# Fourteen of eighteen 128x1024 transposes moved from TensorE to VectorE blocks and DMAs by way of HBM

## The chip, the core and the metric

The kernel runs on one core of a Trainium2 chip. The metric is the device time of one execution in microseconds (us), the median of several runs; lower is better. One further execution was profiled. The engines are named as in the profile: PE is TensorE (PEld its weight loads), DVE is VectorE, ACT is ScalarE, POOL is GpSimd, and SP is the queue from which all of this kernel's DMAs are issued. Each engine and each queue works through its own instructions in the order in which they were written.

## What is computed

Attention without softmax, then a gated MoE layer, then a second MoE layer with SoLU and a layer norm. The change is in the second MoE, for 2304 tokens, a model width of 512 and a hidden width of 1024:

```python
h = x @ w_in                                   # [2304,512] @ [512,1024]
e = np.exp(h - np.max(h, axis=-1, keepdims=True))
sm = e / (np.sum(e, axis=-1, keepdims=True) + 1e-09)
solu = h * sm
mu = np.mean(solu, axis=-1, keepdims=True)
var = np.mean((solu - mu) ** 2, axis=-1, keepdims=True)
ln = (solu - mu) / np.sqrt(var + 1e-06) * g_ln
out = ln @ w_out                               # [2304,1024] @ [1024,512]
```

Everything is float32. A product is made of three matmuls of high and low parts (high by high, high by low, low by high).

## The kernel before

The 2304 tokens are 18 tiles of 128. The first part (attention and the first MoE) leaves its result, transposed, in two SBUF tiles `ya`, one for tokens 0 to 1279 and one for the rest. The second MoE takes the tiles in nine pairs.

For each pair, `make_a` forms the seven left operands of Strassen's product (`A11` to `S4`): four additions on DVE, and for each operand a rounded high part (an ACT copy) and a low part (a POOL subtraction). `run_h` issues the seven products P1 to P7, 42 matmuls of 512 columns in all, and with them, on ACT and DVE, the copies and additions that combine them in PSUM (L942 to L960). A pair occupies two of the four PSUM slots (two banks each).

`post_h` then takes each tile of 128 tokens x 1024 features: DVE finds the maximum (L998), ACT the exponential with its sum (L999), DVE multiplies by h into the SBUF tile `u` (L1000), after which the PSUM slot is free, DVE takes the statistics (L981, L982) and subtracts the mean in place (L1003), and POOL works out the scale of each row (L987 to L992), which the very last step applies.

`run_t` transposes the tile: eight PE transposes of 128x128 (L1020) into another PSUM slot; ACT rounds the result into `dh` (L1029), and DVE subtracts that from it into the low part `dl` (L1030). `dh` and `dl` have two buffers each, the ring `R_D`. `run_o` multiplies with `w_out` (24 matmuls of 512 columns, L703 to L705), ACT scales the rows into `ot`, which has two buffers (L1048), and SP stores it (L1049).

The order of the instructions is made beforehand, by a planner in the kernel's own Python code. The class `Order` keeps a time for each engine; every step has a planned cost in microseconds and a rank, and the step that is due first by these is written next. Nothing of the plan is left when the kernel runs but the order on each engine. The loop of the second MoE chooses what PE does next: a transpose if a tile is due, then the next product of a pair if fewer than `AHEAD` tiles lie between h and out, then the output of a tile:

```python
        if i in d_ready and d_ready[i][0] <= od.now and ps_ready() <= od.now and R_D.ok():
            run_t(todo_t.pop(0))
            continue
        ...
        if h_can and (hp or ahead < AHEAD or not o_can):
            run_h()
            continue
        if o_can:
            run_o(todo_o.pop(0))
```

Of the kernel before, what the change touches and what calls it, by code (L numbers as in the profile page):

```python
# [17 lines left out]
P = 128  # L18
# [120 lines left out]
def attention_moe_moe_kernel(ctx: ExitStack, tc, kv_in, kv_tail, q_in, g_norm, w1, w_in, w_out2, g_ln, out):  # L139
# [224 lines left out]
    def store(k, f, u, su, sf, t, slot=None, raw=None):  # L364

        what, x, y = k

        def free():
            R_U.give(su)
            R_F.give(sf)  # L370
            decode_more()

        if what == "i":

            g, r = x % 2, 2 * (x // 2) + y
# [12 lines left out]
        if what == "o":  # L388

            g = gl_sb[:, x:x + 1]  # L390
            at = raw.bitcast(F32R)
            hi, lo = at[:, 0:CH], at[:, CH:2 * CH]

            def out_to(t):
                free()
                d = scr["o", x] = dr.tile([P, 2 * CH], F32, tag=f"so{x}", name=f"so{x}")
                nc.sync.dma_start(out=d, in_=raw.bitcast(F32))
                scr_at["o", x] = when = od.load(8 * CH * P) + 1.5
                od.chain([(None, 0, gone)], t=when)

            def gone(t):
                R_RAW.give(slot)
                loads()

            od.chain([
                ("T", 1.32, lambda: nc.gpsimd.tensor_tensor(out=f, in0=f, in1=u, op=ALU.add)),
                ("A", 0.7, lambda: nc.scalar.activation(out=hi, in_=f, func=AF.Copy, scale=g)),
                ("S", 0.7, lambda: nc.vector.scalar_tensor_tensor(
                    out=lo, in0=f, scalar=g, in1=hi.bitcast(F32), op0=ALU.mult, op1=ALU.subtract)),
                (None, 0, out_to),  # L410
            ], rank=5, t=t)
# [421 lines left out]

    R_H, R_D, R_AO = Ring(4), Ring(2), Ring(2)
    held, d_ready, dt_ready, scs = [], {}, {}, {}
    G2 = 0.68
    todo_a, todo_h, todo_t, todo_o = list(range(NTT // 2)), list(range(NTT)), list(range(NTT)), list(range(NTT))
    a_ops, a_at = {}, {}  # L840
    AT = {"A11": 0, "A12": 1, "A22": 2, "S1": 3, "S2": 4, "S3": 5, "S4": 6}
    SEQ = [("P1", "A11", B11), ("P6", "S2", T2), ("P2", "A12", B21), ("P5", "S1", T1), ("P7", "S3", T3),
           ("P3", "S4", B22), ("P4", "A22", T4)]
# [10 lines left out]
    def make_a(i, slot, when):  # L854
# [11 lines left out]
        def part(cost, d, src, last):  # L866
            n = slice(*d)

            def done(t):
                for x in range(*d):  # L870
                    a_at[i, x] = t

            od.chain([
                ("A", cost, lambda: nc.scalar.copy(out=hi[:, n], in_=src)),  # L874
                ("G", 2.15 * cost, lambda: nc.gpsimd.tensor_tensor(  # L875
                    out=lo[:, n], in0=src, in1=hi[:, n].bitcast(F32), op=ALU.subtract)),
                (None, 0, done),
            ], rank=2.5, t=max(od.now, last))

        a_ops[i] = at, slot  # L880
        part(0.6, (0, 2), first, when)
# [3 lines left out]
            (None, 0, lambda t: part(0.6, (3, 5), s[:, 0:2], t)),  # L885
            add(s[:, 2], a11, a21, ALU.subtract), add(s[:, 3], a12, s[:, 1], ALU.subtract),
            (None, 0, lambda t: part(0.6, (5, 7), s[:, 2:4], t)),
        ], rank=2.5, t=max(od.now, when))

    hp = []  # L890

    def next_h():

        if not hp:
            i = todo_h[0] // 2 if todo_h else None
            if (i not in a_ops or R_H.taken - len(R_H.given) > 2
                    or sum(t <= od.now for t in ps_free.values()) < 2):
                return INF
            return max([a_at.get((i, 0), INF)] + [b_at.get((g, B11), INF) for g in range(2)])
        p = hp[0]  # L900
# [5 lines left out]
    def run_h():  # L906
        if not hp:
            i = todo_h.pop(0)
            todo_h.pop(0)
            p = {"i": i, "n": 0, "slots": [ps_tile(f"h{i}"), ps_tile(f"h{i + 1}")], "u": [R_H.take(), R_H.take()]}  # L910
            p["a"], p["sa"] = a_ops[i // 2]
            hp.append(p)
        p = hp[0]
# [44 lines left out]
            od.chain([is_done("p7")], t=at)  # L958
        elif name == "P3":
            pre = [("V", 0.69, lambda: nc.vector.tensor_tensor(out=Z, in0=Z, in1=s1, op=ALU.add))]  # L960
            post_or_hold(p["i"], p["slots"][0], p["u"][0], pre)
        elif name == "P4":
            R_AO.give(p["sa"])
            hp.pop()
            post_or_hold(p["i"] + 1, p["slots"][1], p["u"][1], [])
            a_more()

    def post_or_hold(i, slot, sh, pre):
        if ph2 is None:
            held.append(lambda: post_h(i, *slot, sh, pre))  # L970
        else:
            post_h(i, *slot, sh, pre)

    def post_h(i, slot, ps, sh, pre):
        u = ph2.tile([P, 2, 512], F32, tag="u", name=f"u{i}", bufs=4)
        st = ph2.tile([P, 24], F32, tag="st", name=f"st{i}", bufs=6)
        nmax, ssum, mv, sv, sc = st[:, 0:1], st[:, 1:2], st[:, 4:6], st[:, 6:7], st[:, 7:8]

        def stats():
            for n in range(2):  # L980
                nc.vector.bn_stats(out=st[:, 12 + 6 * n:18 + 6 * n], in_=u[:, n, :])  # L981
            nc.vector.bn_aggr(out=mv, in_=st[:, 12:24])  # L982

        def root():


            nc.gpsimd.tensor_scalar(out=ssum, in0=ssum, scalar1=1e-9, scalar2=None, op0=ALU.add)  # L987
            nc.gpsimd.tensor_tensor(out=sv, in0=ssum, in1=ssum, op=ALU.mult)
            nc.gpsimd.tensor_scalar(
                out=sv, in0=sv, scalar1=1e-6, scalar2=mv[:, 1:2], op0=ALU.mult, op1=ALU.add  # L990
            )
            nc.gpsimd.tensor_tensor(out=sc, in0=sv, in1=mhalf[:, 0:1], op=ALU.pow)  # L992

        def ready(t):
            d_ready[i] = (t, u, sh)

        od.chain(pre + [
            ("V", 1.13, lambda: nc.vector.tensor_reduce(out=nmax, in_=ps, axis=AX.XY, op=ALU.max, negate=True)),  # L998
            ("A", 1.09, lambda: nc.scalar.activation(out=u, in_=ps, func=AF.Exp, bias=nmax, accum_out=ssum)),  # L999
            ("V", 1.14, lambda: nc.vector.tensor_tensor(out=u, in0=ps, in1=u, op=ALU.mult)),  # L1000
            ps_done(slot),
            ("V", 1.4, stats),
            ("V", 0.66, lambda: nc.vector.tensor_scalar(  # L1003
                out=u, in0=u, scalar1=mv[:, 0:1], scalar2=None, op0=ALU.subtract)),
            (None, 0, ready),
            ("G", 1.2, root),
            (None, 0, lambda t: scs.__setitem__(i, sc)),
        ], rank=2, t=od.now + 0.2)

    def run_t(i):  # L1010
        _, u, sh = d_ready[i]
        slot, ps = ps_tile(f"t{i}")
        sd = R_D.take()
        u, ps = (x.rearrange("p a f -> p (a f)") for x in (u, ps))
        dh = ph2.tile([P, DF2], F32R, tag="dh", name=f"dh{i}", bufs=2)
        dl = (late[0][0][:, 3584:3584 + DF2], late[0][1][:, 4096:4096 + DF2])[sd % 2]

        def go():
            for ft in range(NF2):
                nc.tensor.transpose(ps[:, ft * P:(ft + 1) * P], u[:, ft * P:(ft + 1) * P], ident)  # L1020

        od.pe(0.87, go)
        R_H.give(sh)

        def done(t):
            dt_ready[i] = (t, dh, dl, sd)

        od.chain([
            ("A", 0.9, lambda: nc.scalar.copy(out=dh, in_=ps)),  # L1029
            ("V", 1.14, lambda: nc.vector.tensor_tensor(out=dl, in0=ps, in1=dh.bitcast(F32), op=ALU.subtract)),  # L1030
            ps_done(slot),
            (None, 0, done),
        ], rank=1.5, t=od.now + 0.2)

    def run_o(i):
        _, dh, dl, sd = dt_ready[i]
# [50 lines left out]
    while any(ab) or busy or yq:  # L1087
# [48 lines left out]
            nxt.append(od.events[0][0])  # L1136
        assert nxt, "stuck"
        od.now = max(od.now, min(nxt))
    AHEAD = 4
    while todo_o:  # L1140
        od.until(od.now)
        late_loads()
# [1 line left out]
        ahead = len(todo_o) - len(todo_h)  # L1144
        h_can = next_h() <= od.now
        i = todo_t[0] if todo_t else None
        if i in d_ready and d_ready[i][0] <= od.now and ps_ready() <= od.now and R_D.ok():
            run_t(todo_t.pop(0))
            continue
        i = todo_o[0]  # L1150
# [78 lines left out]
```

## Time and profile before

| what | value |
|---|---|
| median of three runs | 706.12 us (705.1 to 706.95) |
| the profiled execution, its own time | 706.26 us |
| its span, first to last instruction | 704.5 us |
| mean granted TensorE clock | 0.998 |

The span is shorter than the execution's own time by 1.76 us, which lie outside the first and the last instruction. Busy times are sums over instructions; matmuls are pipelined, so their listed durations overlap, and the time from the start of one step to the start of the next is what a step takes of PE.

### The profile page before, as it was taken

What the parts mean: (1) busy time and instruction counts of PE and PEld (TensorE: products, weight loads), DVE (VectorE), ACT (ScalarE), POOL (GpSimd) and SP (SyncE); (2) the same over time, 40 slices, a digit from 0 to 9 for tenths busy, and PEclk for the clock granted to TensorE, in tenths of its full rate; (3) what the DMA queues carried; (4) which work ended last, traced back from release to release, by engine and by line L of the source; (5) the groups of instructions that cost most, each with busy time, mean ns of one, the idle gap of its engine ahead of it and who ended that gap; (6) DMA issues with size and microseconds to landing.
All of it is one profiled execution on the core that took longest, in us unless ns stands there. A gap on an engine that the chain in (4) does not pass through costs nothing.

```text
span 704.5 us, 9627 instructions
## 1 busy us (share of the span) xinstructions
PE 690.4 (98%) x3690; PEld 600.5 (85%) x3690; DVE 513.3 (73%) x746; ACT 262.0 (37%) x462; POOL 247.5 (35%) x243
## 2 busy tenths in 40 slices
PE   5899999999999999999999999999999999999998
PEld 5799988989898888989898989898788888888887
DVE  2889735888978899779878788565597857765560
ACT  3677534333233233232232232212354534443331
POOL 2676314342364445513232322202335433322110
PEclk9999999999999999999999999999999999999999
DMA  8974101122232121132232312013500000000001
GB/s 295 364 276 143 60 0 61 60 90 90 90 140 99 61 89 60 43 115 83 91 120 76 124 70 91 31 60 122 208 0 31 16 30 31 16 22 24 31 30 46
DMA packets 23630, 61.45 MB, mean 87 GB/s; under 512 B 4768, under 2 KB 6048, under 8 KB 23584
## 3 DMA queue, kind: packets, MB, share of 16 engines
q1 hardware_dynamic: 23584, 60.83, 24.8%
q8 instruction: 29, 0.48, 0.3%
q14 instruction: 17, 0.14, 0.1%
HBM read 48.76 MB, written 12.06 MB: 86 GB/s over the span
## 4 chain that ended last, share of the span: by engine, by line
PE 95%; DMA 3%; SPq 0%; DVE 0%; ACT 0%; issue 0%; ACTq 0%
PE y L788 21%; PE ab L703 14%; PE ab L705 14%; PE ab L704 14%; PE h L928 12%; PE out L705 5%; PE out L703 5%; PE out L704 5%; PE t L1020 2%; DMA kv<-in_kv 2%; PE o L635 2%; DMA raw_w<-in_w 1%; PE t L680 1%; PE pkv L590 1%; SPq L263 0%; DVE ya L801 0%
## 5 line engine op out<-in xcount | busy, mean ns | idle before, releaser
L703 PE MATMUL ab<-xh,wh_w 128*128 128x512 f32 (+1 forms) x480 | 177.9, 371 | 0.0
L705 PE MATMUL ab<-xh,wl_w 128*128 128x512 f32 (+1 forms) x480 | 177.0, 369 | 0.0
L704 PE MATMUL ab<-xl,wh_w 128*128 128x512 f32 (+1 forms) x480 | 176.8, 368 | 0.0
L801 DVE TENSOR_TENSOR ya<-y,ya 128x1024 f32<-128x1024 f32 (+1 forms) x110 | 122.3, 1112 | 2.2 <-PE y L788 2.1
L424 POOL TENSOR_TENSOR f_w<-f_w,wh_w 128x512 f32<-128x512 f32 x36 | 47.8, 1329 | 163.8 <-ACT wh_w L423 106.0
L757 ACT COPY a<-ab 128x512 f32<-128x512 f32 (+1 forms) x60 | 32.7, 544 | 193.8 <-PE ab L705 193.7
L758 DVE TENSOR_TENSOR ab<-ab,a 128x512 f32<-128x512 f32 (+1 forms) x60 | 38.7, 646 | 85.0 <-ACT a L757 84.8
L703 PEld LDWEIGHTS ab<-xh,wh_w 128*128 128x128 f32 x480 | 90.1, 188 | 12.2 <-issue 0.3
L704 PEld LDWEIGHTS ab<-xl,wh_w 128*128 128x128 f32 x480 | 90.2, 188 | 11.6
L705 PEld LDWEIGHTS ab<-xh,wl_w 128*128 128x128 f32 x480 | 90.1, 188 | 11.4
L788 PE MATMUL y<-gl,wh_w 128*128 128x512 f32 (+1 forms) x240 | 88.5, 369 | 0.3 <-DVE gl L760 0.3
L788 PE MATMUL y<-gh,wh_w 128*128 128x512 f32 (+1 forms) x240 | 88.8, 370 | 0.0
L788 PE MATMUL y<-gh,wl_w 128*128 128x512 f32 (+1 forms) x240 | 88.5, 369 | 0.0
L928 PE MATMUL h<-wd,lateh 128*128 128x512 f32 x216 | 58.1, 390 | 0.0
L788 PEld LDWEIGHTS y<-gl,wh_w 128*128 128x128 f32 x240 | 45.1, 188 | 6.6 <-DVE gl L760 0.8
L788 PEld LDWEIGHTS y<-gh,wh_w 128*128 128x128 f32 x240 | 45.1, 188 | 5.8
L788 PEld LDWEIGHTS y<-gh,wl_w 128*128 128x128 f32 x240 | 45.0, 188 | 5.6
L425 POOL TENSOR_TENSOR wl_w<-f_w,u_w 128x512 fp32r<-128x512 f32 x36 | 47.6, 1327 | 3.6 <-DVE u_w L345 2.2
L928 PEld LDWEIGHTS h<-wd,lateh 128*128 128x128 f32 x216 | 40.5, 188 | 8.4
L928 PE MATMUL h<-latel,lateh 128*128 128x512 f32 x162 | 46.3, 394 | 0.0
L703 PE MATMUL out<-wh_o,dh 128*128 128x512 f32 (+1 forms) x114 | 43.9, 385 | 0.0
L875 POOL TENSOR_TENSOR lateh<-ya,lateh 128x512 fp32r<-128x512 f32 (+1 forms) x18 | 18.2, 1016 | 72.6 <-ACT lateh L874 72.6
(103 smaller groups left out, 1141.7 us busy)
## 6 DMA issues: line engine op xcount, KB each, us to landing
raw_w<-in_w SPq DMA_DIRECT2D x36, 512.0 KB, 3.4
kv<-in_kv SPq DMA_DIRECT2D x16, 512.0 KB, 7.1
out<-ot SPq DMA_DIRECT2D x17, 256.0 KB, 2.0
raw_i<-in_w_in SPq DMA_DIRECT2D x8, 512.0 KB, 3.5
raw_o<-in_w_out SPq DMA_DIRECT2D x8, 512.0 KB, 3.3
so<-raw_o SPq DMA_DIRECT2D x8, 512.0 KB, 2.6
q<-in_q SPq DMA_DIRECT2D x12, 256.0 KB, 5.1
si<-wd SPq DMA_DIRECT2D x6, 512.0 KB, 2.6
```

The lines of the kernel that those rows point to most:

```text
L424: ("T", 1.32, lambda: nc.gpsimd.tensor_tensor(out=f, in0=f, in1=hi.bitcast(F32), op=ALU.subtract)),
L425: ("T", 1.38, lambda: nc.gpsimd.tensor_tensor(out=lo, in0=f, in1=u, op=ALU.add)),
L635: nc.tensor.matmul(ps[m * w:(m + 1) * w, p * P:(p + 1) * P], lhsT=src[:, m * w:(m + 1) * w], rhs=bds[b % 2][:, p], start=True, stop=True)
L703: nc.tensor.matmul(o, lhsT=ah, rhs=bh, start=first, stop=False)
L704: nc.tensor.matmul(o, lhsT=ah, rhs=bl, start=False, stop=False)
L705: nc.tensor.matmul(o, lhsT=al, rhs=bh, start=False, stop=last)
L757: ("A", 0.45 * k, lambda: nc.scalar.copy(out=a, in_=ps[:, 0, 0:nb])),
L758: ("V", 0.54 * k, lambda: nc.vector.tensor_tensor(out=g, in0=g, in1=a, op=ALU.mult)),
L788: nc.tensor.matmul(o, lhsT=x[:, s], rhs=y, start=f == fs[0] and n == 0, stop=f == fs[-1] and n == 2)
L801: op = ("V", 0.9 * nb / NB, lambda: nc.vector.tensor_tensor(out=dst, in0=src, in1=dst, op=ALU.add))
L875: ("G", 2.15 * cost, lambda: nc.gpsimd.tensor_tensor(out=lo[:, n], in0=src, in1=hi[:, n].bitcast(F32), op=ALU.subtract)),
L928: nc.tensor.matmul(o, lhsT=x, rhs=y, start=first and k == m == 0, stop=k == 1 and m == 2, skip_group_check=not first)
```

## The change

For tiles 4 to 17 (all but those in `ON_PE`) the PE transpose goes. In its place:

- DVE transposes the tile `u` in 32x32 blocks, in two instructions of 128x512, into a piece of `ya` that is no longer needed (each pair's piece joins the list `ya_free` when all seven of its operands are made). The input is read at a step of four elements.
- SP issues two stores of this piece to HBM and, behind them, two loads from there, which bring the tile back with the blocks in their transposed places: 256 KB each, in runs of 512 bytes. A load goes to another free piece of `ya`, or to `u` if none is free. The planner counts 6.0 us (`HOP`) from the stores to the data.
- ACT and DVE make `dh` and `dl` from this SBUF tile instead of from PSUM; no PSUM slot is taken.

For all 18 tiles the mean is subtracted by ACT (as mean minus value, and `g_ln` is negated once by POOL to make up for it), not by DVE. `u` is taken from its four buffers only at the exponential, and no longer at the start of the pair. `AHEAD` is 6, not 4. The making of the operands has rank 1.7 in place of 2.5, now ahead of the steps of `post_h`, which have rank 2 and a little more for each tile.

```diff
+            minus = ("G", 0.3, lambda: nc.gpsimd.tensor_scalar(out=gl_sb, in0=gl_sb, scalar1=-1.0, scalar2=None, op0=ALU.mult))
+            od.chain([minus] * (x == 0) + [
...
+    NU, PLACES = 4, 2
+    R_H, R_D, R_AO = Ring(NU), Ring(2), Ring(2)
...
+    ya_free, HOP, ON_PE = [], 6.0, (0, 1, 2, 3)
...
+                if all((i, x) in a_at for x in range(7)):
+                    ya_free.append(i)
...
-            ], rank=2.5, t=max(od.now, last))
+            ], rank=1.7, t=max(od.now, last))
...
-            if (i not in a_ops or R_H.taken - len(R_H.given) > 2
-                    or sum(t <= od.now for t in ps_free.values()) < 2):
+            if i not in a_ops or sum(t <= od.now for t in ps_free.values()) < PLACES:
...
+        def go(t):
+            if not R_H.ok():
+                od.chain([(None, 0, go)], rank=2 + 0.02 * i, t=t + 0.2)
+                return
+            sh = R_H.take()
+            u = ph2.tile([P, 2, 512], F32, tag="u", name=f"u{i}", bufs=NU)
...
+            uf = u.rearrange("p a f -> p (a f)")
+            st_u = {}
+            def blocks(h):
+                n = slice(h * 4, h * 4 + 4)
+                nc.vector.transpose(out=ya_of(st_u["b"]).rearrange("p b (f i) -> p f b i", i=32)[:, n],
+                                    in_=uf.rearrange("p (f i b) -> p f b i", b=4, i=32)[:, n])
+            def turn(t):
+                if i in ON_PE:
+                    d_ready[i] = (t, uf, lambda: R_H.give(sh))
+                    return
+                if not ya_free:
+                    od.chain([(None, 0, turn)], rank=2 + 0.02 * i, t=t + 0.2)
+                    return
+                st_u["b"] = ya_free.pop(0)
+                st_u["d"] = [dr.tile([P, 4 * P], F32, tag=f"su{i % 4}{h}", name=f"su{i}_{h}") for h in range(2)]
+                ops = []
+                for h in range(2):
+                    ops += [("V", 0.6, lambda h=h: blocks(h)), (None, 0, lambda t, h=h: off(t, h))]
+                od.chain(ops, rank=2 + 0.02 * i, t=t)
+            def off(t, h):
+                nc.sync.dma_start(out=st_u["d"][h].rearrange("p (b e) -> p b e", b=4),
+                                  in_=ya_of(st_u["b"])[:, :, h * P:(h + 1) * P])
+                if h:
+                    back_in(t)
+            def back_in(t):
+                od.chain([(None, 0, lambda t: ya_free.append(st_u["b"]))], t=t + 2.3)
+                if ya_free:
+                    n = ya_free.pop(0)
+                    to = ya_of(n)
+                    R_H.give(sh)
+                    free = lambda: ya_free.append(n)
+                else:
+                    to = uf.rearrange("p (a e) -> p a e", a=4)
+                    free = lambda: R_H.give(sh)
+                for h in range(2):
+                    nc.sync.dma_start(out=to[:, :, h * P:(h + 1) * P],
+                                      in_=st_u["d"][h].rearrange("(a j) (b e) -> (j b) a e", a=4, b=4))
+                d_ready[i] = (t + HOP, to, free)
...
+                ("A", 1.25, lambda: nc.scalar.activation(out=u, in_=ps, func=AF.Exp, bias=nmax, accum_out=ssum)),
+                ("V", 1.2, lambda: nc.vector.tensor_tensor(out=u, in0=ps, in1=u, op=ALU.mult)),
+                ps_done(slot),
+                ("V", 1.5, stats),
+                ("A", 1.09, lambda: nc.scalar.activation(out=u, in_=u, func=AF.Identity, bias=mv[:, 0:1], scale=-1.0)),
+                (None, 0, turn),
...
-            ("V", 0.66, lambda: nc.vector.tensor_scalar(
-                out=u, in0=u, scalar1=mv[:, 0:1], scalar2=None, op0=ALU.subtract)),
...
+        if i in ON_PE:
...
+        else:
+            src, freed = u.rearrange("p a (f i) -> p f a i", i=32), (None, 0, lambda t: free())
+            to = [d.rearrange("p (f a i) -> p f a i", a=4, i=32) for d in (dh, dl)]
...
+            ("A", 1.05, lambda: nc.scalar.copy(out=to[0], in_=src)),
+            ("V", 1.2, lambda: nc.vector.tensor_tensor(out=to[1], in0=src, in1=to[0].bitcast(F32), op=ALU.subtract)),
...
-    AHEAD = 4
+    AHEAD = 6
...
-        if i in d_ready and d_ready[i][0] <= od.now and ps_ready() <= od.now and R_D.ok():
+        if i in d_ready and d_ready[i][0] <= od.now and R_D.ok() and (i not in ON_PE or ps_ready() <= od.now):
```

## Rows read from the trace of the kernel before

**Rows 1.** The page: engine, busy us, share of the span, instructions.

```profile
PE 690.4 (98%) x3690; PEld 600.5 (85%) x3690; DVE 513.3 (73%) x746; ACT 262.0 (37%) x462; POOL 247.5 (35%) x243
```

**Rows 2.** The page, the chain that ended last, by engine.

```profile
PE 95%; DMA 3%; SPq 0%; DVE 0%; ACT 0%; issue 0%; ACTq 0%
```

**Rows 3.** Stretches: window, length, busy us by engine, granted clock, DMA share, GB/s.

```profile
500.40:565.00 64.60, 64.56 (x304) 53.35 (x303) 52.14 (x75) 31.05 (x51) 28.11 (x41) 1.00 0.10 37
565.00:690.00 125.00, 125.00 (x606) 104.62 (x605) 76.58 (x109) 49.41 (x74) 33.16 (x60) 1.00 0.07 26
587.50:609.70 22.20, 22.20 (x107) 18.55 (x106) 14.46 (x22) 9.69 (x15) 7.46 (x12) 1.00 0.07 25
690.00:704.50 14.50, 11.24 (x73) 10.08 (x71) 1.23 (x1) 2.68 (x5) 0.00 (x0) 1.00 0.15 54
```

**Rows 4.** The chain in order of time, one pair: start us, us, what.

```profile
572.69 9.54 PE h L928 x42
...
587.68 0.87 PE t L1020 x8
588.55 0.23 PE out L703
...
594.02 0.87 PE t L1020 x8
594.89 9.54 PE h L928 x42
```

**Rows 5.** Groups on DVE by form, 150 to 480 us: 128x512 from SBUF.

```profile
L345 DVE SCALAR_TENSOR_TENSOR u_w<-raw_w,u_w 128x512 f32<-128x512 uint32 x24 | 20.6, 860 | 0.3
...
L341 DVE TENSOR_SCALAR u_o<-f_o 128x512 uint32<-128x512 uint32 x8 | 3.4, 420 | 0.0
```

**Rows 6.** Groups on DVE, 505 to 692 us: busy us, mean ns, idle before.

```profile
L981 DVE BATCH_NORM_STATS2 st<-u 128x6 f32<-128x512 f32 x36 | 22.7, 671 | 0.0
L1003 DVE TENSOR_SCALAR u<-u,st 128x1024 f32<-128x1024 f32 x18 | 13.0, 728 | 0.0
L1030 DVE TENSOR_TENSOR latel<-t,dh 128x1024 fp32r<-128x1024 f32 x9 | 11.0, 1220 | 5.6 <-ACT dh L1029 5.5
L864 DVE TENSOR_TENSOR bt<-ya,bt 128x256 f32<-128x256 f32 x7 | 4.0, 574 | 0.0
L864 DVE TENSOR_TENSOR bt<-bt,ya 128x256 f32<-128x256 f32 x7 | 2.9, 419 | 0.0
```

**Rows 7.** Groups on ACT, the whole span.

```profile
L999 ACT ACTIVATE u<-h,st 128x1024 f32<-128x1024 f32 x18 | 20.1, 1118 | 12.3 <-DVE st L998 12.2
L1029 ACT CAST dh<-t 128x1024 fp32r<-128x1024 f32 x18 | 18.3, 1019 | 6.6 <-PE t L1020 5.1
...
L874 ACT CAST lateh<-bt 128x512 fp32r<-128x512 f32 x18 | 11.2, 624 | 20.7 <-DVE bt L864 20.5
...
L324 ACT ACT_TABLE_LOAD x1 | 1.3, 1283 | 0.7 <-PEq L1219 0.7
```

**Rows 8.** The SP queue in order of time: start us, us of issuing, instruction.

```profile
19.44 2.01 SPq L256 DMA_DIRECT2D qs<-in_q  x2
...
500.43 0.32 SPq L511 DMA_DIRECT2D wh_o<-so  x1
```

**Rows 9.** DMA issues: count, KB each, median us from issue to landing.

```profile
out<-ot SPq DMA_DIRECT2D x17, 256.0 KB, 2.0
...
so<-raw_o SPq DMA_DIRECT2D x8, 512.0 KB, 2.6
...
wh_o<-so SPq DMA_DIRECT2D x6, 256.0 KB, 2.7
...
qs<-in_q SPq DMA_DIRECT2D x4, 128.0 KB, 8.1
```

**Rows 10.** Stretches of the first part: columns as in Rows 3.

```profile
5.00:10.00 5.00, 3.10 (x42) 2.56 (x44) 2.67 (x5) 1.23 (x4) 1.37 (x2) 1.00 0.98 361
45.00:50.00 5.00, 5.00 (x38) 4.96 (x36) 4.01 (x5) 4.16 (x11) 4.53 (x3) 1.00 0.99 359
```

**Rows 11.** DVE in order of time behind one pair: start us, us, instruction.

```profile
603.84 2.36 DVE L998 TENSOR_REDUCE st<-h 128x1 f32<-128x1024 f32 x2
...
611.54 0.70 DVE L1003 TENSOR_SCALAR u<-u,st 128x1024 f32<-128x1024 f32 x1
```

More of the change, by code (lines that the diff above doesn't have):

```diff
@@ L403, in gone @@
                 loads()
-            od.chain([
+            minus = ("G", 0.3, lambda: nc.gpsimd.tensor_scalar(out=gl_sb, in0=gl_sb, scalar1=-1.0, scalar2=None, op0=ALU.mult))
+            od.chain([minus] * (x == 0) + [
                 ("T", 1.32, lambda: nc.gpsimd.tensor_tensor(out=f, in0=f, in1=u, op=ALU.add)),
@@ L830, in second @@
         held.clear()
-    R_H, R_D, R_AO = Ring(4), Ring(2), Ring(2)
+    NU, PLACES = 4, 2
+    R_H, R_D, R_AO = Ring(NU), Ring(2), Ring(2)
     held, d_ready, dt_ready, scs = [], {}, {}, {}
@@ L887, in make_a @@
             (None, 0, lambda t: part(0.6, (5, 7), s[:, 2:4], t)),
-        ], rank=2.5, t=max(od.now, when))
+        ], rank=1.7, t=max(od.now, when))
     hp = []
@@ L909, in run_h @@
             todo_h.pop(0)
-            p = {"i": i, "n": 0, "slots": [ps_tile(f"h{i}"), ps_tile(f"h{i + 1}")], "u": [R_H.take(), R_H.take()]}
+            p = {"i": i, "n": 0, "slots": [ps_tile(f"h{i}"), ps_tile(f"h{i + 1}")]}
             p["a"], p["sa"] = a_ops[i // 2]
@@ L960, in run_h @@
             pre = [("V", 0.69, lambda: nc.vector.tensor_tensor(out=Z, in0=Z, in1=s1, op=ALU.add))]
-            post_or_hold(p["i"], p["slots"][0], p["u"][0], pre)
+            post_or_hold(p["i"], p["slots"][0], pre)
         elif name == "P4":
@@ L964, in run_h, with post_or_hold @@
             hp.pop()
-            post_or_hold(p["i"] + 1, p["slots"][1], p["u"][1], [])
+            post_or_hold(p["i"] + 1, p["slots"][1], [])
             a_more()
-    def post_or_hold(i, slot, sh, pre):
+    def post_or_hold(i, slot, pre):
         if ph2 is None:
-            held.append(lambda: post_h(i, *slot, sh, pre))
+            held.append(lambda: post_h(i, *slot, pre))
         else:
[L972 to L976, printed above, removed]
+            post_h(i, *slot, pre)
@@ L977, in post_h @@
+    def post_h(i, slot, ps, pre):
+        st = ph2.tile([P, 24], F32, tag="st", name=f"st{i}", bufs=8)
         nmax, ssum, mv, sv, sc = st[:, 0:1], st[:, 1:2], st[:, 4:6], st[:, 6:7], st[:, 7:8]
[L979 to L992, printed above, removed]
@@ L994, in ready, with stats, root @@
-        def ready(t):
-            d_ready[i] = (t, u, sh)
-        od.chain(pre + [
[L998 to L1002, printed above, removed]
-            ("V", 0.66, lambda: nc.vector.tensor_scalar(
-                out=u, in0=u, scalar1=mv[:, 0:1], scalar2=None, op0=ALU.subtract)),
[L1005 to L1008, printed above, removed]
+        def go(t):
[4 more added lines that the diff above has]
+            u = ph2.tile([P, 2, 512], F32, tag="u", name=f"u{i}", bufs=NU)
+            def stats():
+                for n in range(2):
+                    nc.vector.bn_stats(out=st[:, 12 + 6 * n:18 + 6 * n], in_=u[:, n, :])
+                nc.vector.bn_aggr(out=mv, in_=st[:, 12:24])
+            def root():
+                nc.gpsimd.tensor_scalar(out=ssum, in0=ssum, scalar1=1e-9, scalar2=None, op0=ALU.add)
+                nc.gpsimd.tensor_tensor(out=sv, in0=ssum, in1=ssum, op=ALU.mult)
+                nc.gpsimd.tensor_scalar(
+                    out=sv, in0=sv, scalar1=1e-6, scalar2=mv[:, 1:2], op0=ALU.mult, op1=ALU.add
+                )
+                nc.gpsimd.tensor_tensor(out=sc, in0=sv, in1=mhalf[:, 0:1], op=ALU.pow)
+            uf = u.rearrange("p a f -> p (a f)")
[36 more added lines that the diff above has]
+                d_ready[i] = (t + HOP, to, free)
+            od.chain([
+                ("A", 1.25, lambda: nc.scalar.activation(out=u, in_=ps, func=AF.Exp, bias=nmax, accum_out=ssum)),
[4 more added lines that the diff above has]
+                (None, 0, turn),
+                ("G", 1.2, root),
+                (None, 0, lambda t: scs.__setitem__(i, sc)),
+            ], rank=2 + 0.02 * i, t=t)
@@ L1010, in run_t, with ya_of @@
+        od.chain(pre + [
+            ("V", 1.2, lambda: nc.vector.tensor_reduce(out=nmax, in_=ps, axis=AX.XY, op=ALU.max, negate=True)),
+            (None, 0, go),
+        ], rank=2 + 0.02 * i, t=od.now + 0.2)
+    def ya_of(i):
+        hf, c = half(2 * i * P)
+        return ya[hf][:, :, c:c + 2 * P]
     def run_t(i):
-        _, u, sh = d_ready[i]
-        slot, ps = ps_tile(f"t{i}")
+        _, u, free = d_ready[i]
         sd = R_D.take()
-        u, ps = (x.rearrange("p a f -> p (a f)") for x in (u, ps))
@@ L1015, in run_t, with go @@
         dh = ph2.tile([P, DF2], F32R, tag="dh", name=f"dh{i}", bufs=2)
         dl = (late[0][0][:, 3584:3584 + DF2], late[0][1][:, 4096:4096 + DF2])[sd % 2]
[L1018 to L1023, printed above, removed]
+        if i in ON_PE:
+            slot, ps = ps_tile(f"t{i}")
+            src, to, freed = ps.rearrange("p a f -> p (a f)"), (dh, dl), ps_done(slot)
+            def go():
+                for ft in range(NF2):
+                    nc.tensor.transpose(src[:, ft * P:(ft + 1) * P], u[:, ft * P:(ft + 1) * P], ident)
+            od.pe(0.87, go)
+            free()
+        else:
+            src, freed = u.rearrange("p a (f i) -> p f a i", i=32), (None, 0, lambda t: free())
+            to = [d.rearrange("p (f a i) -> p f a i", a=4, i=32) for d in (dh, dl)]
@@ L1028, in run_t @@
         od.chain([
-            ("A", 0.9, lambda: nc.scalar.copy(out=dh, in_=ps)),
-            ("V", 1.14, lambda: nc.vector.tensor_tensor(out=dl, in0=ps, in1=dh.bitcast(F32), op=ALU.subtract)),
-            ps_done(slot),
+            ("A", 1.05, lambda: nc.scalar.copy(out=to[0], in_=src)),
+            ("V", 1.2, lambda: nc.vector.tensor_tensor(out=to[1], in0=src, in1=to[0].bitcast(F32), op=ALU.subtract)),
+            freed,
             (None, 0, done),
-        ], rank=1.5, t=od.now + 0.2)
+        ], rank=1.5, t=od.now + 0.2 * (i in ON_PE))
     def run_o(i):
```

## The prediction, before the result was known

> **What bounds the kernel now.** I read the page first: PE is busy for 690.4 of 704.5 us, and no other engine for more than 73% [rows 1]. A busy PE need not be the limit, so the chain of work that ended last comes next: PE holds 95% of it, DMA 3% (the first loads), and DVE and ACT round to nothing [rows 2]. POOL does not occur in it. Last I cut the second MoE, which starts at 500.4 us, into stretches. From 565 to 690 us PE is busy for all 125 us at a granted clock of 1.00, and in the 65 us before that it lacks 0.04 us; only at the end, where the last scaling and the last store follow the last matmul, does it idle for 3.3 us [rows 3]. So in the stage that the change touches, no wait of PE exists that could be shortened: the time falls by the work taken from PE, and rises by whatever wait is new.
>
> The stage repeats in pairs of 22.20 us. The chain splits one pair: 9.54 us for the 42 matmuls of h, two transposes of 0.87 us, and 5.47 us for each of the two outputs (594.02 less 588.55) [rows 4]; that makes 9.54 + 1.74 + 10.94 = 22.22 us. In the same 22.20 us DVE is busy for 14.46, ACT for 9.69, POOL for 7.46 us, and the DMA engines for 7% [rows 3].
>
> **What it removes.** Fourteen transposes of 0.87 us, which lie on the path with nothing beside them: 14 x 0.87 = 12.2 us. A pair without transposes takes 22.20 - 1.74 = 20.46 us of PE.
>
> **What it adds on DVE.** Two block transposes of 128x512 for each tile. The trace before holds none. The nearest rows for the cost of 512 elements in and out of SBUF are a tensor_scalar at 0.42 us and a two-input operation at 0.86 us [rows 5]; between them lies the statistics instruction, which like a transpose reads one 128x512 operand, at 0.67 us [rows 6]. I take 0.67 and keep 0.42 and 0.86. The subtraction of 0.73 us goes. Per pair: 14.46 - 2 x 0.73 + 4 x 0.67 = 15.7 us of 20.46, or 77% (14.7 to 16.4 at the ends). The low part `dl` now has both inputs in SBUF. At the least it stays at 1.22 us; additions of the same size with both inputs in SBUF take 0.42 us in one place of the plan and 0.57 in another [rows 6], and that ratio would make it 1.67, another 0.9 us per pair, 17.3 us in all at the worst, 85%. DVE still has room, so these costs lie beside PE. If that cover were gone, each microsecond above 20.46 would count once per pair, seven times.
>
> **What it adds on ACT.** The subtraction of the mean has the shape of the exponential, whose instruction takes 1.12 us [rows 7]: 9.69 + 2.24 = 11.9 us per pair, 58%. The copy into `dh` takes 1.02 us from PSUM; from SBUF it is bounded above by two casts of 0.62 us [rows 7], which adds 0.4 us per pair. ACT loads a function table once in the whole span, at 1.28 us [rows 7]. If the new function needed another table, two loads per tile would add 5.1 us per pair; 17.4 of 20.46 us would still fit. For the first four tiles the subtraction only changes engines, 0.73 us there against 1.12 here, in a stretch where DVE is busy 52.1 of 64.6 us and ACT 31.1 [rows 3].
>
> **What it adds on SP.** Four DMAs per tile of 512 runs each. The two loads of `qs` that have as many runs took 2.01 us of issuing together, a load with one run per partition 0.32 us [rows 8], so between 1.3 and 4.0 us of SP per tile, and I take 4.0. The wait is new: a load from HBM must wait on SP until its store has landed. Landing took 2.0 to 2.7 us for DMAs of this size or twice it in the quiet parts, and 8.1 us for `qs` while the first loads crowded the engines [rows 9]. With a landing L, SP is held for 1.0 (first issue), L less what overlaps, and the last issue, L + 2.0 us in all, and 0.3 for the store of the output: 5.0 us at L = 2.7, 10.4 us at L = 8.1, against a period of 10.23 us per tile. I take 2.7, since the engines stand at 7% in this stage. The new traffic is 1 MB per tile. In a stretch with runs of 256 bytes among others the engines moved 359 GB/s at a share of 0.99, no less than the 361 GB/s of one at 0.98 before them [rows 10], so 1 MB needs 2.9 us of the engines per tile. Their share should go from 0.07 to about 0.35.
>
> What stands behind that wait on SP: the second load, the next tile's stores and the outputs. An output held back holds an `ot` buffer, which ACT needs only two tiles later, some 20 us. Behind a late load waits the copy into `dh` on ACT, behind it the copies of the h products, and for those waits PE. So how late may the data be? Stores and loads, one behind the other, take 2 x 2.7 + 2 x 1.0 = 7.4 us, or 18.2 us at 8.1 each; the plan allows 6.0. With `AHEAD` at 6 the loop, in its steady state, starts a pair when five tiles lie between h and out, and then writes two outputs. The copy of a pair's first tile is due, by the ring `R_D`, after four outputs and one further pair, 4 x 5.47 + 9.54 = 31.4 us after that pair's last matmul. The maximum to the subtraction takes 8.4 us for both tiles now (603.84 to 612.24) [rows 11]; 0.4 for ACT's longer subtraction and four transposes at 0.67 make some 11.5 us. That leaves 20 us for a hop of 7 to 18: hidden at both ends, with little left at the upper one.
>
> **The rest.** The negation of `g_ln` is one small POOL instruction in the first part, at worst a microsecond on an engine that the chain does not hold, and at best nothing. The ranks, the later taking of `u` and the PSUM slots set free only change the order on engines with room; they can lose nothing while PE waits for none of them, and can gain nothing, since PE has no wait to lose. If that cover failed it would show as PE waits inside the h products. At the end more outputs follow the last h than before, so the last tiles' data have longer; the final 3.3 us stay.
>
> **The sum.** From the profiled execution's own time: 706.26 - 12.2 = 694.1 us, if nothing new is exposed. That execution lies 0.14 us above the median of the runs. The first hop and the change from the PE tiles to the others are where the plan has least to draw on; I add 0.9 us, an estimate of about one DVE instruction of 128x1024 exposed once, not in each pair, and predict 695.0 us. A change within 0.3%, 2.1 us, is about what a measurement of this kernel cannot tell from none.
>
> **Rivals.**
>
> *DVE too late for the h products.* PE needs two additions of DVE inside each pair. With DVE at 77 to 85% such an addition more often finds the engine taken by an instruction of up to 1.2 us. Half of that, at both places, in seven pairs costs 2 x 0.6 x 7 = 8.4 us and gives 702.5; a part of it anything from 698. For it speaks that the first stretch already has DVE at 81% [rows 3]; against it, that PE waits for nothing even there. Chance 0.13. Its extreme, DVE as the bound of the pair, begins at transposes of (20.46 - 13.0) / 4 = 1.86 us.
>
> *Given back in full.* If the new waits on ACT and SP add up to 0.87 us per tile, the time stays within 704 to 708 us. It takes several small lapses in each tile. Chance 0.06.
>
> *The SP queue paces the stage: slower.* The place is the load waiting for its store. The queue is full from L + 2.3 = 10.23, L = 7.9 us, and the kernel is slower than before from a period of 11.1 us, L = 8.8 us. At L = 12 it would cost 14 x (14.3 - 11.1) = 45 us, 751 us. For it: 8.1 us was seen. Against it: only beside full engines. Chance 0.09.
>
> *The rearranged load is broken into single elements: slower by far.* The stores and loads do the transpose by their addresses. Were they moved as 4-byte pieces, a load would have 65,536 of them; at the pace of 256-byte pieces, 359 GB/s over 16 engines or 11.4 ns each [rows 10], that is 47 us per load, 93 per tile, 1,300 us over fourteen tiles, some 1,850 us in all. Against it: both sides have runs of 512 bytes, twice those of `qs`. Chance 0.04. The Trainium skill, "VectorE: DVE Perf Modes", section "The three transpose paths", speaks against this change: a plain DMA that transposes by strides is given there as 19 times slower than the crossbar's when the innermost step at the destination is large. Taken onto a load of 2.7 us that would be an estimated 51 us, so the sum would be of the same order as this rival's; here the innermost step is one element, and no row before shows such a DMA.
>
> **How the numbers follow.** The forecast has 0.68, with its own range from 692.8 (no exposure, and 1.3 us for the spread of runs) to 698. The first rival's 0.13 lies mostly below 702; with that the range 692.8 to 702 holds about 0.8. Faster by more than 0.3% is the forecast and the first rival, 0.81; within it 0.06; slower the last two, 0.13.
>
> **What would show it.** Right: a steady pair of 20.5 us with PE busy throughout, eight transposes left in each of four tiles only, DVE at 15 to 17 us per pair, block transposes near 0.67 us, landings under 4 us, DMA at a third, and no PE wait on ACT's `dh` or DVE's `dl`. Wrong: PE idle inside h behind DVE (the first rival), ACT waiting on a DMA at the `dh` copy with PE idle behind it, or SP waiting without a break.

## The result, and the profile after

The kernel became faster, from 705.95 to 695.69 us in the median; the ratio is 0.9857, with a 95% interval of 0.9837 to 0.9877. The profiled execution took 695.12 us, with a span of 693.3.

The page after, with the engines' busy times and the chain by engine, against [rows 1, 2]:

```profile
PE 676.4 (98%) x3578; PEld 586.8 (85%) x3578; DVE 531.6 (77%) x756; ACT 277.7 (40%) x480; POOL 247.5 (36%) x244
...
PE 92%; DVE 4%; DMA 2%; issue 1%; ACT 1%; SPq 1%; DVEq 0%; ACTq 0%
```

PE has 14.0 us less, 12.0 of them in the second MoE, and still holds the chain, but DVE, which rounded to nothing there, now has 4% of it. The stretches, with the columns of [rows 3]:

```profile
500.40:565.00 64.60, 63.33 (x295) 52.07 (x294) 53.01 (x75) 37.68 (x59) 28.80 (x44) 1.00 0.19 59
565.00:690.00 125.00, 124.32 (x569) 103.16 (x568) 93.31 (x118) 60.23 (x87) 31.77 (x58) 1.00 0.44 133
587.50:609.70 22.20, 22.20 (x99) 18.38 (x99) 20.88 (x28) 12.09 (x19) 9.74 (x14) 1.00 0.62 182
```

PE lacks 1.27 us in the first stretch and 0.68 in the second, where it lacked 0.04 and nothing. In the third, DVE is busy for 20.88 of 22.20 us where it was 14.46. The chain in order of time has two steady pairs, against [rows 4]:

```profile
580.69 9.52 PE h L932 x42
601.09 9.52 PE h L932 x42
```

From one h to the next pass 20.40 us, where it was 22.20. The third stretch above is as long as a pair of before, and so longer than a pair now. One of the new pairs, and four of them in a row:

```profile
580.69:601.09 20.40, 20.40 (x92) 16.89 (x91) 19.45 (x25) 12.72 (x19) 10.00 (x16) 1.00 0.44 131
580.69:662.29 81.60, 81.60 (x361) 67.23 (x360) 71.07 (x91) 43.78 (x63) 26.57 (x49) 1.00 0.43 130
```

Per pair DVE is busy for 17.8 us in the mean of the four; three of them have 19.0 to 19.5 us and one 13.1.

The stage itself can be compared without the first part: from the first weight load of h (500.2 us before, 499.1 after) to the end of the span it took 204.3 us before and 194.2 after. In it PE is busy for 12.0 us less, about the 12.2 of the transposes, and idle for 1.9 us more. The rest of the difference between the two spans, 1.1 us, lies in the first part, where the change adds no more than the POOL instruction on `g_ln`; from 18 to 24 us the granted clock was 0.72 in the execution before and 1.00 in the one after. Below, "the stage" is always this length, in the profiled execution.

Groups of instructions after, against [rows 6, 7]:

```profile
L1010 DVE STREAM_TRANSPOSE ya<-u 128x512 f32<-128x512 f32 x28 | 29.0, 1073 | 0.0
...
L1053 ACT ACTIVATE u<-u,st 128x1024 f32<-128x1024 f32 x18 | 20.5, 1153 | 5.2 <-DVE st L992 5.1
...
L1092 ACT CAST dh<-ya 128x1024 fp32r<-128x1024 f32 x14 | 14.6, 1040 | 0.0
...
L1093 DVE TENSOR_TENSOR latel<-ya,dh 128x1024 fp32r<-128x1024 f32 x7 | 9.1, 1295 | 14.2 <-ACT dh L1092 14.2
```

A block transpose took 1.07 us, not 0.67. The others are where they were expected. The DMA issues and the SP queue in order of time, against [rows 8, 9]:

```profile
su<-ya SPq DMA_DIRECT2D x28, 256.0 KB, 2.7
ya<-su SPq DMA_DIRECT2D x28, 256.0 KB, 3.0
```
```profile
661.17 2.46 SPq L1028 DMA_DIRECT2D su<-ya  x3
663.78 2.38 SPq L1044 DMA_DIRECT2D ya<-su  x2
...
667.56 3.45 SPq L1044 DMA_DIRECT2D ya<-su  x2
```

A store lands in 2.7 us and a load in 3.0. The last pair's eight DMAs leave SP between 661.17 and 671.01 us, so the last data are there at about 674. The waits of PE (what waited for whom: us in total, times, longest), and the two places in order of time:

```profile
PE t L1080 <- ACT u L1053: 1.3, 2, 1.0
...
PE h L932 <- DVE h L946: 0.7, 1, 0.7
```
```profile
521.05 1.09 PE L1080 MATMUL t<-ident,u 128*128 128x128 f32 x8 [0.95 <-ACT u L1053]
```
```profile
569.89 3.07 DVE L1010 STREAM_TRANSPOSE ya<-u 128x512 f32<-128x512 f32 x3
572.85 0.69 DVE L946 TENSOR_TENSOR h<-h,bt 128x512 f32<-128x512 f32 x1
```

The first two transposes on PE wait for the subtraction that moved to ACT, and one addition that a product of h needs stands behind three block transposes.

ACT itself waited for DVE at the first of those two. The additions that make operands (L864 before, L867 after) between the first tile's maximum and the end of its statistics, before and after, and the subtraction behind them:

```profile
511.87 0.42 DVE L864 TENSOR_TENSOR bt<-ya 128x256 f32<-128x256 f32 x1
515.25 0.21 DVE L982 BATCH_NORM_AGGREGATE st<-st 128x2 f32<-128x12 f32 x1
```
```profile
509.57 0.81 DVE L867 TENSOR_TENSOR bt<-ya 128x256 f32<-128x256 f32 x1
511.44 0.41 DVE L867 TENSOR_TENSOR bt<-bt,ya 128x256 f32<-128x256 f32 x1
513.51 1.41 DVE L867 TENSOR_TENSOR bt<-ya 128x256 f32<-128x256 f32 x1
516.15 0.21 DVE L992 BATCH_NORM_AGGREGATE st<-st 128x2 f32<-128x12 f32 x1
516.39 1.15 ACT L1053 ACTIVATE u<-u,st 128x1024 f32<-128x1024 f32 x1 [1.27 <-DVE st L992]
```

With 2.6 us of additions in front, where it was 0.4, the statistics end 17.3 us after the stage's start, where they ended after 15.3.

### The profile page after: what moved, and what is told of

Its sections match the earlier page's. It is cut to its first block, busy times and chain, and to the rows that moved or that the text cites. A ratio compares the mean times of both kernels' runs of the same rounds, so it can differ in the third digit from the quotient of the medians.

```text
span 693.3 us, 9568 instructions
## 1 busy us (share of the span) xinstructions
PE 676.4 (98%) x3578; PEld 586.8 (85%) x3578; DVE 531.6 (77%) x756; ACT 277.7 (40%) x480; POOL 247.5 (36%) x244
## 4 chain that ended last, share of the span: by engine, by line
PE 92%; DVE 4%; DMA 2%; issue 1%; ACT 1%; SPq 1%; DVEq 0%; ACTq 0%
PE y L789 21%; PE ab L704 14%; PE ab L706 14%; PE ab L705 14%; PE h L932 10%; PE out L704 4%; PE out L705 4%; PE out L706 4%; DMA kv<-in_kv 2%; PE o L636 2%; PE t L681 1%; PE pkv L591 1%; DVE st L991 1%; SPq L263 1%; DVE ya L1010 1%
## 5 line engine op out<-in xcount | busy, mean ns | idle before, releaser
L704 PEld LDWEIGHTS ab<-xh,wh_w 128*128 128x128 f32 x480 | 90.2, 188 | 12.2 <-issue 0.3
L705 PE MATMUL out<-wl_o,dh 128*128 128x512 f32 (+1 forms) x114 | 43.1, 378 | 0.0
```

The costliest lines, as they stand in the source:

```text
L704: nc.tensor.matmul(o, lhsT=ah, rhs=bh, start=first, stop=False)
L705: nc.tensor.matmul(o, lhsT=ah, rhs=bl, start=False, stop=False)
```

## The experiments

The lines of the edits are against the changed kernel.

**All transposes on PE again.**

```diff
-    ya_free, HOP, ON_PE = [], 6.0, (0, 1, 2, 3)
+    ya_free, HOP, ON_PE = [], 6.0, tuple(range(18))
```

> All 18 tiles are transposed by PE again; the rest of the change (subtraction on ACT, six tiles ahead, the ranks, the later taking of u) stays. If the gain is the work taken from PE less some 2 us of new PE waits: 14 transposes of 0.87 us come back and the 0.7 us that PE waited for DVE inside a pair goes, 695.7 + 12.2 - 0.7 = 707.2 us (706 to 708.5). Rival, the new order has a share in the gain: under 705 us. Rival, the new order costs more than it seems to: over 709 us.

707.18 us, a ratio to the kernel before of 1.0014 (1.0002 to 1.0026); the stage 205.5 us. The transposes' place is the whole gain. What else the change does (subtraction on ACT, six tiles ahead, the ranks) has no gain by itself and costs about 1 us, and the 1.3 us of PE waiting for ACT are still in this trace while the 0.7 us for DVE are gone.

**No hop.** The stores and loads are left out.

```diff
             def off(t, h):
+                if h:
+                    R_H.give(sh)
+                    d_ready[i] = (t, ya_of(st_u["b"]), lambda: ya_free.append(st_u["b"]))
+                return
```

> The stores to HBM and the loads back are left out; dh and dl are made from the block-transposed piece itself, so the 128x128 transposes are not completed and the output is not the reference's. If the hop lies hidden behind the tiles ahead: 694.5 to 696 us, no change beyond the spread. Rival, some of the hop or of its DMA traffic (a share of 0.44 of the engines) is exposed: under 694 us. Rival, the order is better with the delay: over 697 us.

696.25 us, ratio 0.9855 (0.9835 to 0.9876), the stage 194.3 us against 194.2, with the same PE waits of 1.3 and 0.7 us. The hop and its 14.7 MB cost nothing. (The planner counts no time for a hop here, so part of the order differs as well.)

**A block transpose by itself.**

```diff
+    by4 = lambda x: x[:, 0:512].rearrange("p (f i b) -> p f b i", b=4, i=32)
+    runs = lambda x: x.rearrange("p (b f i) -> p f b i", b=4, i=32)[:, 0:4]
+    flat = lambda x: x[:, 0:512].rearrange("p (f b i) -> p f b i", b=4, i=32)
...
+    for _ in range(4):
+        nc.vector.transpose(out=runs(w), in_=by4(m))
+    for _ in range(4):
+        nc.vector.transpose(out=flat(w), in_=by4(m))
+    for _ in range(4):
+        nc.vector.transpose(out=runs(w), in_=flat(m))
+    for _ in range(4):
+        nc.vector.transpose(out=w[:, 0:512], in_=m[:, 0:512])
+    for _ in range(4):
+        nc.vector.transpose(out=w.bitcast(BF)[:, 0:512], in_=m.bitcast(BF)[:, 0:512])
+    for _ in range(4):
+        nc.vector.tensor_copy(out=runs(w), in_=by4(m))
+    for _ in range(4):
+        nc.vector.tensor_copy(out=w[:, 0:512], in_=m[:, 0:512])
```

> The changed kernel with 28 DVE instructions of 128x512 behind its end, on two scratch buffers, four of each form, so that each is measured with the other engines idle; the time of the kernel itself says nothing. If a block transpose of 4-byte elements goes at half the pace of an element per cycle: every fp32 form near 1.07 us, whatever its steps, and the 2-byte form near 0.6 us. Rival, the step of four elements in the input costs the second half: 1.07 us with that step, about 0.6 us without. Rival, other engines slow it in the kernel: all forms about 0.6 us here.

The groups on DVE behind the kernel's end; by line, the transposes are those of the edit in its order, then the two copies. L1238 is the change's own form, which reads at a step of four and writes runs of 32 elements that lie apart; L1240 reads at a step of four and writes side by side; L1242 reads side by side and writes such runs; L1244 has neither, and L1246 is the same in bf16.

```profile
L1238 DVE STREAM_TRANSPOSE m<-m 128x512 f32<-128x512 f32 x4 | 4.5, 1133 | 0.1
L1240 DVE STREAM_TRANSPOSE m<-m 128x512 f32<-128x512 f32 x4 | 4.4, 1096 | 0.1
L1244 DVE STREAM_TRANSPOSE m<-m 128x512 f32<-128x512 f32 x4 | 2.8, 712 | 0.1
L1246 DVE STREAM_TRANSPOSE m<-m 128x512 bf16<-128x512 bf16 x4 | 2.8, 712 | 0.1
L1242 DVE STREAM_TRANSPOSE m<-m 128x512 f32<-128x512 f32 x4 | 2.8, 711 | 0.1
L1248 DVE COPY m<-m 128x512 f32<-128x512 f32 x4 | 2.4, 612 | 0.1
L1250 DVE COPY m<-m 128x512 f32<-128x512 f32 x4 | 1.7, 427 | 0.1
```

The first rival is right: the step of four in the input makes 0.71 us into 1.10. With the input side by side the width of an element makes no difference, nor do runs of 32 in the output; the other engines do not slow it in the kernel (1.07 there, 1.13 here). An output at a step of single elements was not tried. A copy with the change's steps takes 0.61 us, and 0.43 without.

**The transposes read side by side.** The host lays out the rows of `w_out` and `g_ln` in the matching order.

```diff
-                                    in_=uf.rearrange("p (f i b) -> p f b i", b=4, i=32)[:, n])
+                                    in_=uf.rearrange("p (f b i) -> p f b i", b=4, i=32)[:, n])
...
+            pv, uw = ps, u
+            if i in ON_PE:
+                pv = ps.rearrange("p a f -> p (a f)").rearrange("p (f b j) -> p f b j", b=4, j=32)
+                uw = uf.rearrange("p (f j b) -> p f b j", b=4, j=32)
...
+            bits("moe2_w_out").reshape(NF2, 4, 32, DM).transpose(0, 2, 1, 3)).reshape(NF2, P, DM),
...
+            np.asarray(inputs["moe2_g_ln"]).reshape(NF2, 4, 32).transpose(2, 1, 0)).reshape(P, NF2),
```

> The block transposes read 32 elements that lie side by side, not at a step of four; the rows of w_out and the entries of g_ln are laid out in the matching order, and for the four tiles on PE the exponential and the product write u in that order. The planner's costs stay. If the step costs the difference as in the measurement by itself: 0.71 us per transpose, DVE at about 19.4 us where it was 20.9, the 0.7 us of PE waiting for DVE goes, 695.0 us (694.4 to 695.6). Rival, the transposes stay near 1.07 us in the kernel because of the other engines: 695.7 us.

695.82 us, ratio 0.985 (0.9835 to 0.9865); the stage 193.8 us against 194.2. The transposes took 0.69 us, and in the stretch from 587.5 us DVE was busy for 17.98 us, not 20.88, but the time did not move beyond the spread. The wait for DVE went, and of PE's waits 1.0 us for ACT before a transpose stayed, with a new one of 0.5 us for an ACT copy inside h. That copy stood behind an exponential of one of the four PE tiles, which this edit writes at a step of four, at 2.1 us in place of 1.1 (the product into `u` takes 2.0 in place of 1.2):

```profile
509.61 2.07 ACT L1053 ACTIVATE u<-h,st 128x1024 f32<-128x1024 f32 x1 [0.40 <-DVE st L1064]
511.53 0.58 ACT L950 COPY bt<-h 128x512 f32<-128x512 f32 x1
```

So of the 10.8 us that the transposes save, DVE keeps 7.4 over the stage (140.2 us against 147.6), and the edit brings a wait of its own in place of the one that it removes. Seven microseconds less of DVE are worth nearly nothing here: DVE was full in places, but not the bound.

**Each block transpose twice,** unknown to the planner, and then counted by it (the second with `("V", 2.1, ...)`).

```diff
                 nc.vector.transpose(out=ya_of(st_u["b"]).rearrange("p b (f i) -> p f b i", i=32)[:, n],
                                     in_=uf.rearrange("p (f i b) -> p f b i", b=4, i=32)[:, n])
+                nc.vector.transpose(out=ya_of(st_u["b"]).rearrange("p b (f i) -> p f b i", i=32)[:, n],
+                                    in_=uf.rearrange("p (f i b) -> p f b i", b=4, i=32)[:, n])
```

> Each block transpose is issued twice, into the same place; the planner counts it once. DVE then has about 4.3 us more per pair. If DVE at 20.9 of 22.2 us in the dense stretch is nearly a second bound: 25 us of DVE against pairs of 20.4 us of PE there, PE waits show in several pairs, 700 to 708 us. Rival, DVE has the room that was forecast (77%): under 697.5 us.

> Each block transpose is issued twice, as before, which made 723.7 us, but now the planner counts both (2.1 us). If DVE's amount of work is the second bound (176 of some 190 us in the stage): still 716 us or more. If what cost 28 us was the order, planned without those 30 us of DVE: 700 to 712 us.

723.7 us (ratio 1.0241, 1.0215 to 1.0268) and 721.68 us (1.0212, 1.0193 to 1.0231). The 30 us more of DVE raise the stage from 194.2 to 221.3 and 221.9 us, 27 of 30 either way, much more than was expected of the first. Whether the planner knows of the work only moves the waits: unknown, PE waited 10.5 us for the additions inside h; counted, 10.4 us for `dh` before outputs. From 565 to 690 us DVE was busy for 114.6 and 120.3 of 125 us, where it was 93.3. This shows how near the second bound lies. Not all of the 27 us are waits: the granted clock fell with PE's pauses, to means of 0.93 and 0.95 in that stretch, and over the stage PE was busy for 9 us more in both, and idle for 18 us more.

**The planner told the measured cost.**

```diff
-                    ops += [("V", 0.6, lambda h=h: blocks(h)), (None, 0, lambda t, h=h: off(t, h))]
+                    ops += [("V", 1.08, lambda h=h: blocks(h)), (None, 0, lambda t, h=h: off(t, h))]
```

> The planner counts 1.08 us for a block transpose, as measured, instead of 0.6; the work is the same, its order on the engines changes. If the wait of PE for DVE inside a pair (0.7 us) comes from an order that was made with too low a cost: it goes, 695.0 us (694.5 to 695.6). Rival, the order was right by luck and the new one makes PE wait elsewhere: 696 us and more.

700.23 us, ratio 0.9915 (0.9902 to 0.9929): slower than the changed kernel by 4.5 us, the stage by 3.4. My theory held for the wait inside h, which went, but at the end PE waited 1.8 us for `dh` and 0.5 for `dl`, and the clock fell behind that. ACT there, in order of time, and the clock in two stretches:

```profile
679.64 0.69 ACT L1111 ACTIVATE ot<-out,st 128x512 f32<-128x512 f32 x1 [4.75 <-PE out L706]
680.23 1.98 ACT L1092 CAST dh<-ya 128x1024 fp32r<-128x1024 f32 x2
```
```profile
680.00:685.00 5.00, 3.16 (x10) 2.19 (x11) 2.36 (x2) 2.21 (x3) 0.00 (x0) 0.85 0.16 59
685.00:690.00 5.00, 5.00 (x22) 4.18 (x21) 0.00 (x0) 0.37 (x1) 0.00 (x0) 0.81 0.00 0
```

The `dh` copies stand behind the scaling of an output, and this waits for PE, so PE, done with that output, must wait for both. I first put this down to the hop, whose last loads were issued at 674.8 us there.

**The same order without the DMAs.**

```diff
                 if h:
                     back_in(t)
-                nc.sync.dma_start(out=st_u["d"][h].rearrange("p (b e) -> p b e", b=4),
-                                  in_=ya_of(st_u["b"])[:, :, h * P:(h + 1) * P])
...
-                    nc.sync.dma_start(out=to[:, :, h * P:(h + 1) * P],
-                                      in_=st_u["d"][h].rearrange("(a j) (b e) -> (j b) a e", a=4, b=4))
```

> The kernel of e4_cost (700.2 us) without the stores to HBM and the loads back; the order of all other instructions on every engine is the same, and dh and dl are made from what the destination held before, so the output is not the reference's. In e4_cost the last pair's loads were issued as late as 674.8 us and ACT's last two dh copies ran only at 680.2 us, with PE idle before them. If the exposed hop of the last pair is what made that order slow: 696 to 697.5 us. Rival, the order itself, with DVE and ACT late: 699 us and more.

698.7 us, ratio 0.9898 (0.9876 to 0.9919), the stage 196.0 us against 197.6 with the DMAs. It lies between the two forecasts, and the trace decides: ACT in the same place,

```profile
678.58 0.69 ACT L1105 ACTIVATE ot<-out,st 128x512 f32<-128x512 f32 x1 [4.75 <-PE out L706]
679.17 1.98 ACT L1086 CAST dh<-ya 128x1024 fp32r<-128x1024 f32 x2
```

and PE's waits are the same 1.8 and 0.5 us. So the exposed hop is not the cause; it is the order, in which the copies were written behind an output's scaling. In the two profiled stages PE is idle for the same 6.9 us, and the granted clock stayed at 1.00 here, so the clock is the difference between them. It does not go with the DMAs alone: the mean clock of this kernel's four executions was 0.998 in three and 0.993 in the slowest, 700.54 us, and 0.992 to 0.995 in all five with the DMAs. Why it fell in the one and not in the other stays open.

**The subtraction of the four PE tiles back on DVE.**

```diff
-                ("A", 1.09, lambda: nc.scalar.activation(out=u, in_=u, func=AF.Identity, bias=mv[:, 0:1], scale=-1.0)),
+                ("A", 1.09, lambda: nc.scalar.activation(out=u, in_=u, func=AF.Identity, bias=mv[:, 0:1], scale=-1.0))
+                if i not in ON_PE else ("V", 0.66, lambda: nc.vector.tensor_scalar(
+                    out=u, in0=u, scalar1=mv[:, 0:1], scalar2=-1.0, op0=ALU.subtract, op1=ALU.mult)),
```

> For the four tiles that PE transposes the mean is subtracted by DVE again (with the sign of the change); for the other fourteen by ACT. If the 1.3 us that PE waits for ACT before two transposes are the price of that move: they go, 694.4 us (693.8 to 695.2). Rival, DVE is as full there and PE waits for it instead: 695.5 us and more.

702.28 us, ratio 0.9941 (0.9926 to 0.9955), the stage 199.8 us. The 1.3 us of PE waiting for ACT went, with 0.5 of waiting for DVE before transposes in their place, but the whole order changed with them: DVE was busy for 19.90 of 20 us from 565 to 585 us and PE for 16.43, and PE waited, among others, 2.8 us for the product into `u` before an output. The price of the move to ACT cannot be read from the time, since the edit reorders everything behind it. The first tile, in front of which the order is still the same, tells something:

```profile
517.62 0.74 DVE L1054 TENSOR_SCALAR u<-u,st 128x1024 f32<-128x1024 f32 x1
```

Its subtraction ends 18.2 us after the stage's start (500.17 us here), against 18.4 with ACT, and 17.0 in the kernel before.

**Four tiles ahead.**

```diff
-    AHEAD = 6
+    AHEAD = 4
```

> AHEAD is 4 again, all else as in the changed kernel. A tile's copy is then due after two outputs and one pair, 20.5 us after its pair's last matmul, for a chain of some 13 us and a hop of 7 to 10. If the tiles ahead are what hides the hop: ACT waits for loads at the dh copy and PE behind it, 699 to 705 us. Rival, four tiles hide it as well: under 697 us.

711.56 us, ratio 1.0074 (1.0051 to 1.0098), the stage 209.2 us: slower even than the kernel before. The end of the chain in order of time:

```profile
679.62 1.01 DVE ya L1010
681.27 1.47 SPq L1112
682.79 2.69 DMA su<-ya
685.97 3.30 DMA su<-ya
689.28 3.12 DMA ya<-su
692.48 1.05 ACT dh L1092
693.58 0.79 PE out L704
```

With four tiles ahead the last tile's hop lies open, 12 us from its block transpose to the copy: PE waits 8.1 us for that `dh`, ACT 10.1 us for loads in four places, and the mean granted clock from 680 to 710 us is 0.83.

**A faster version.** Side by side as above, with the planner told of 0.72 us for a transpose and 8.0 us for the hop, and two PE tiles instead of four.

```diff
-    ya_free, HOP, ON_PE = [], 6.0, (0, 1, 2, 3)
+    ya_free, HOP, ON_PE = [], 8.0, (0, 1)
```

> The block transposes read side by side (as e10_contig), the planner counts 0.72 us for one and 8.0 us for the hop, and only the first two tiles are transposed by PE. If PE stays the bound: two more transposes of 0.87 us go, 694.0 us (693.3 to 695). Rival, the two tiles are needed earlier than their hop ends, so PE waits for them: 695.7 us and more.

693.43 us, ratio 0.9827 (0.9806 to 0.9848), the stage 191.8 us, 2.4 less than with the change: 1.7 for the two transposes, the rest from waits. Its interval and that of the changed kernel overlap at the edge, so the step beyond the change is likely but not certain; against the kernel before it is clear.

## Why the prediction was right, and where not

- **The bound and the term removed** were right. PE was the path, 14 x 0.87 = 12.2 us came off it, and a steady pair takes 20.40 us, forecast 20.46. With all transposes on PE the gain is gone. The total, 695.69 us, lies 0.7 us from the forecast. That is about what the exposed remainder came out larger than the 0.9 us that I added.
- **DVE's addition was mis-sized.** I took 0.67 us for a block transpose and bounded it by 0.42 and 0.86; it took 1.07, outside the bounds. All the rows that I compared read their input side by side or at a step of two; this one reads at a step of four, and by itself that is worth 0.38 us. So DVE came to 17.8 us per pair in the mean, and 19.0 to 19.5 in dense ones, not 15.7, above the worst that I allowed, 17.3; the transposes are 1.6 us of the 2.1. (The 20.88 us above, from which the forecast for the doubled transposes also starts, belong to a stretch of 22.20 us, longer than a pair now.) Of this only the 0.7 us of one late addition show in the total, because DVE was still not the path: with 0.69 us per transpose the time is the same within its spread. But the margin was nearly used up, as the doubled transposes show.
- **The exposed remainder** was 1.9 us, not 0.9, and not at the first hop or the change from the PE tiles, where I put it. 1.3 of it lies before the first two transposes on PE, where the trace of before shows PE going from h to the transposes without a pause. I had costed both the move of the subtraction to ACT and the new ranks at nothing there, the ranks because they "can lose nothing while PE waits for none of them". The traces point to the ranks: with the making of the operands now first, the statistics of the first tile come 2.0 us later and those of the second 1.7, and with the first tile's subtraction back on DVE, behind the same additions, it ended only 0.2 us sooner. No run changes the rank alone, so this is read from the traces and not tested. 0.7 is the first rival's mechanism, an addition for h behind three block transposes, once and not in seven pairs.
- **The hop** was as forecast: landings of 2.7 and 3.0 us, issuing of 0.53 us for a store and 0.37 for a load (medians) instead of 1.0, and 7 to 8 us from the first store's issue to the last landing, 9.4 and 10.7 for the second tile of the last two pairs. No `dh` copy of ACT waited for a load. Leaving the hop out changes nothing, and four tiles ahead instead of six bares it. The forecast of 20 us of room was for the steady state; at both ends of the stage it was less: about 1 us for the second tile that takes the hop (data at 565.6 us, its copy at 566.8) and less than 6 for the last one (data at 674 us, the copy at 679.67 in this line of ACT):

```profile
679.67 1.04 ACT L1092 CAST dh<-ya 128x1024 fp32r<-128x1024 f32 x1
```

- **The rivals.** SP never paced the stage. The loads were not broken up: they land in 3.0 us. The Trainium skill's rule ("VectorE: DVE Perf Modes", section "The three transpose paths") would by my estimate have made it 51. That rule speaks of a large innermost step, and here 512 bytes lie together, so this case does not contradict it. The DMA engines' share rose to 0.44, not 0.35.

## What to carry to other kernels

When one engine is the whole path, moving work off it pays nearly in full (10.1 of 12.2 us here) as long as the receiving engine has room and the new latency falls behind work already lined up; here two more tiles of lookahead were what made a round trip by way of HBM free, and they have to reach to the last tile. Price an instruction with the steps of its access pattern, not by its size alone. And where the order comes from a greedy plan, a truer cost need not give a better order: each edit of a cost is a new order, to be measured as such.

## What the runs showed of the hardware that was not expected

- A DVE block transpose of 128x512 takes 0.71 us in fp32 and in bf16 alike with the input side by side, and 1.10 us with a step of four fp32 elements.
- ACT's exponential of 128x1024 from PSUM takes 1.12 us with its output side by side, and 2.07 us with its output at a step of four fp32 elements.
- DMAs of 512 runs of 512 bytes between SBUF and HBM land in 2.7 us (store) and 3.0 us (load), close to the 2.0 to 2.7 us of those with longer runs.
- With PE waits of 1.85 and 0.53 us that ended at 681.3 and 682.6 us, the granted clock was 0.85 from 680 to 685 us and 0.81 from 685 to 690 in one kernel, part of the time at the lower of its two levels, and 1.00 with the same waits in the profiled execution of another.
